# Attention with the keys on the partitions, transposed output, sums by additions and ones, a gate by tanh

## The chip, the cores and the metric

The kernel runs on one core of a Trainium2 chip. The time is the device time in microseconds (us) of that core; the median of several runs is quoted. Engine names in the profile: PE is TensorE's matmuls, PEld its weight loads, DVE is VectorE, ACT is ScalarE, POOL is GpSimd. "Cold" means that the profile shows TensorE's clock at half (0.50), "warm" at full (1.00). A "strip" is half of the rows or half of the columns of TensorE's array (64*128 or 128*64 in the profile, where the whole is 128*128). A "pass" is one streaming of 384 columns through the array, 0.16 us when warm (the p of the prediction): one for a bf16 matmul, four for an fp32 one, which runs as two parts of 0.32 us. Ratios of two kernels are the mean time of one kernel's fast runs over that of the other's fast runs of the same rounds, so they are not quite the ratio of the quoted medians.

## The reference

Two blocks in a row, all in fp32. Attention has 4 batches, 8 heads, 768 positions and 64 columns per head; a key counts for a query only if six sign bits of a projection agree:

```
q_bits = (einsum(q, proj) > 0);  k_bits = (einsum(k, proj) > 0)      # 6 bits each
mask   = bucket(q_bits) == bucket(k_bits)
scores = where(mask, q @ k.T / 8, -1e9)
attn   = exp(scores - max) / (sum + 1e-9)
x      = attn @ v                     # regrouped to 3072 tokens x 512
g = x @ w_gate;  val = x @ w_val      # 512 -> 1536
out = (g * sigmoid(g) * val) @ w_out  # 1536 -> 512
```

The three weights come as float64 and are rounded to fp32 on the chip ("narrowing": 36 pieces of 128 x 512, seven VectorE operations each).

## The kernel before

Heads are taken in pairs; a pair's q and k lie transposed with one head on partitions 0 to 63 and the other on 64 to 127. A unit of attention is 128 queries of one head, with the queries on the partitions. Its weights come out with queries on the partitions, so they must be turned (transposed) before they can be multiplied with the values, and the result must be turned again for the gated block. The mask is a matmul of the hash bits (bf16) added to the scores in PSUM.

```python
    def score(u):
        n, c, h = units[u]
        rows = slice(h * D, (h + 1) * D)
        ...
        for half in range(2):
            nc.tensor.matmul(sc[:, half, 0:HQ], bits["q", n][rows, qs], bits["k", n][rows, ks], start=True, stop=False)
            nc.tensor.matmul(sc[:, half, 0:HQ], T["q", n][rows, qs], T["k", n][rows, ks], start=False, stop=True)
        nc.vector.tensor_reduce(top, sc[:, :, 0:HQ], axis=AX.XY, op=ALU.max)
        ...  # scale and bias from top, two small operations
        nc.scalar.activation(A[u], sc[:, :, 0:HQ], AF.Exp, bias=bias, scale=scale, accum_out=sums[u])

    def turn(u):      # six transposes, copied out by VectorE and ScalarE
        ...
    def attend(u):    # six matmuls: turned weights stationary, 64 columns of values moving
        for i in range(NCH):
            nc.tensor.matmul(ps[:, 0:D], at[:, i, :], raws["v", n][:, h, i, :], start=i == 0, stop=i == NCH - 1)
        ...  # reciprocal of the sum, scaling
    def x_T(n, c):    # one transpose per two units, copied into xT
        ...
        # the gated block, per 128 of the 1536 columns
        def up(f):
            ...  # g and val: four fp32 matmuls of 384 columns each
            nc.scalar.copy(gs, g[:, 0:HQ])
            nc.scalar.activation(e, g[:, 0:HQ], AF.Exp, scale=-1.0)
            nc.vector.tensor_scalar(e, e, scalar1=1.0, scalar2=None, op0=ALU.add)
            nc.vector.reciprocal(e, e)
            nc.vector.tensor_tensor(gs, gs, e, op=ALU.mult)
            nc.vector.tensor_tensor(ht, gs, val[:, 0:HQ], op=ALU.mult)
```

Batch 0's attention runs while the weights are narrowed; the gated block of a batch runs in small pieces among the attention units of the next batch; the last batch's block stands alone at the end.

## Time and profile before

The median of before is 1792.73 us (1784.3 to 1793.24, three runs). I mark three stretches by the start of each batch's first g matmul:

| stretch of the profiled run | before, us |
|---|---|
| start to the first g (batch 0's attention, weights narrowed) | 385.5 |
| first g to the last batch's first g, per batch | 400.1 |
| last batch's first g to the end | 204.9 |

The sum 385.5 + 3 x 400.1 + 204.9 is the span of 1790.7. The last stretch still holds the end of attention in this kernel: a batch's block comes in two halves, and the second half of the last one starts at 1614.69. The prediction below shows the page's lines and reads them. The first stretch is cold nearly throughout, so a matmul removed there is worth about twice what it is worth later.

### The profile page before, as it was taken

What the parts mean: (1) busy time and instruction counts of PE and PEld (TensorE: products, weight loads), DVE (VectorE), ACT (ScalarE), POOL (GpSimd) and SP (SyncE); (2) the same over time, 40 slices, a digit from 0 to 9 for tenths busy, and PEclk for the clock granted to TensorE, in tenths of its full rate; (3) what the DMA queues carried; (4) which work ended last, traced back from release to release, by engine and by line L of the source; (5) the groups of instructions that cost most, each with busy time, mean ns of one, the idle gap of its engine ahead of it and who ended that gap; (6) DMA issues with size and microseconds to landing.
All of it is one profiled execution on the core that took longest, in us unless ns stands there. A gap on an engine that the chain in (4) does not pass through costs nothing.

```text
span 1790.7 us, 18403 instructions
## 1 busy us (share of the span) xinstructions
PE 1745.6 (97%) x7136; PEld 1111.1 (62%) x7136; DVE 1054.9 (59%) x2247; ACT 395.0 (22%) x793; POOL 19.8 (1%) x42
## 2 busy tenths in 40 slices
PE   6999999999999999999999999999999999999999
PEld 4677676766665666566665666566665666565454
DVE  6888887346652666346653666356653566256272
ACT  1111121112221222222221222122222222121010
POOL 0000000000000000000000000000000000000000
PEclk7555555569999999999999999999999899999999
DMA  5222221100001100020002000020001000000000
GB/s 143 84 80 77 80 77 36 27 1 10 1 1 47 25 1 1 12 51 10 0 1 62 10 1 1 12 51 10 1 6 39 1 1 0 12 7 0 18 1 18
DMA packets 63416, 45.23 MB, mean 25 GB/s; under 512 B 51552, under 2 KB 55648, under 8 KB 63328
## 3 DMA queue, kind: packets, MB, share of 16 engines
q1 hardware_dynamic: 58144, 25.18, 5.5%
q0 software_dynamic: 5184, 18.88, 3.6%
q8 instruction: 56, 0.92, 0.2%
q14 instruction: 32, 0.26, 0.1%
HBM read 37.75 MB, written 6.29 MB: 25 GB/s over the span
## 4 chain that ended last, share of the span: by engine, by line
PE 95%; DVE 2%; ACT 1%; issue 0%; DMA 0%; SPq 0%; ACTq 0%; DVEq 0%
PE av L241 17%; PE sc L206 16%; PE g L273 15%; PE po L289 14%; PE val L273 13%; PE aps L228 9%; PE sc L204 5%; PE hps L173 4%; PE tps L165 2%; PE xps L257 1%; ACT AT L234 1%; DVE e L280 1%; DMA kraw<-in_k_dram 0%; DVE ht L283 0%; DVE AT L232 0%
## 5 line engine op out<-in xcount | busy, mean ns | idle before, releaser
L241 PEld LDWEIGHTS av<-vraw,AT 128*128 128x128 f32 x2304 | 338.1, 224 | 70.9 <-issue 38.5
L206 PE MATMUL sc<-kT,qT 64*128 64x384 f32 x768 | 370.7, 569 | 0.0
L241 PE MATMUL av<-vraw,AT 128*128 128x64 f32 x2304 | 336.1, 305 | 2.6 <-DVE AT L232 2.6
L219 ACT ACTIVATE A<-sc,bias,scale 128x768 f32<-128x768 f32 x192 | 190.3, 991 | 618.4 <-DVE bias L215 528.0
L209 DVE TENSOR_REDUCE top<-sc 128x1 f32<-128x768 f32 x192 | 183.8, 958 | 192.6 <-PE sc L206 191.9
L273 PE MATMUL g<-xT,wg 128*128 128x384 f32 x768 | 272.6, 499 | 0.0
L273 PE MATMUL val<-xT,wv 128*128 128x384 f32 x768 | 263.4, 486 | 0.0
L289 PE MATMUL po<-wo,ht 128*128 128x512 f32 x576 | 250.8, 593 | 0.0
L280 DVE RECIPROCAL e<-e 128x384 f32<-128x384 f32 x96 | 245.1, 2553 | 3.3
L273 PEld LDWEIGHTS g<-xT,wg 128*128 128x128 f32 x768 | 144.2, 193 | 108.1 <-issue 23.3
L273 PEld LDWEIGHTS val<-xT,wv 128*128 128x128 f32 x768 | 146.1, 190 | 102.2 <-issue 0.9
L206 PEld LDWEIGHTS sc<-kT,qT 64*128 64x128 f32 x768 | 162.1, 222 | 56.3 <-issue 56.3
L228 PE MATMUL aps<-ident,A 128*128 128x128 f32 x1152 | 189.0, 309 | 3.1 <-ACT A L219 3.1
L289 PEld LDWEIGHTS po<-wo,ht 128*128 128x128 f32 x576 | 108.6, 190 | 132.5 <-issue 129.8
L248 DVE TENSOR_SCALAR xn<-av,r 128x64 f32<-128x64 f32 x192 | 54.5, 284 | 213.5 <-PE av L241 195.3
L234 ACT COPY AT<-aps 128x384 f32<-128x384 f32 x192 | 91.5, 477 | 402.0 <-PE aps L228 401.8
L279 DVE TENSOR_SCALAR e<-e 128x384 f32<-128x384 f32 x96 | 34.5, 360 | 231.3 <-ACT e L278 231.3
L228 PEld LDWEIGHTS aps<-ident,A 128*128 128x128 f32 x1152 | 161.2, 173 | 3.7 <-ACT A L219 3.7
L204 PE MATMUL sc<-kb,qb 64*128 64x384 bf16 x384 | 142.3, 371 | 0.2 <-DVE kb L178 0.2
L232 DVE COPY AT<-aps 128x384 f32<-128x384 f32 x192 | 105.8, 551 | 5.1 <-PE aps L228 3.9
L204 PEld LDWEIGHTS <-qb 64*128 64x128 bf16 x384 | 38.6, 100 | 72.1 <-issue 47.3
L276 ACT COPY gs<-g 128x384 f32<-128x384 f32 x96 | 45.9, 478 | 138.6 <-PE g L273 138.6
(59 smaller groups left out, 809.3 us busy)
## 6 DMA issues: line engine op xcount, KB each, us to landing
qraw<-in_q_dram SPq DMA_DIRECT2D x32, 192.0 KB, 3.5
words<-in_moe_w_gate_dram POOLq DMA_DIRECT2D x12, 512.0 KB, 3.8
kraw<-in_k_dram SPq DMA_DIRECT2D x32, 192.0 KB, 4.2
vraw<-in_v_dram SPq DMA_DIRECT2D x16, 384.0 KB, 4.0
words<-in_moe_w_val_dram POOLq DMA_DIRECT2D x12, 512.0 KB, 3.9
words<-in_moe_w_out_dram POOLq DMA_DIRECT2D x12, 512.0 KB, 3.8
out_dram<-o SPq DMA_DIRECT2D x24, 256.0 KB, 2.0
proj<-in_proj_dram SPq DMA_DIRECT2D x2, 1.5 KB, 3.4
```

Source lines behind the costliest of these rows:

```text
L173: nc.tensor.matmul(ps[:, 0:HQ], proj2, T[name, n][:, cols], start=True, stop=True)
L204: nc.tensor.matmul(sc[:, half, 0:HQ], bits["q", n][rows, qs], bits["k", n][rows, ks], start=True, stop=False)
L206: nc.tensor.matmul(sc[:, half, 0:HQ], T["q", n][rows, qs], T["k", n][rows, ks], start=False, stop=True)
L209: nc.vector.tensor_reduce(top, sc[:, :, 0:HQ], axis=AX.XY, op=ALU.max)
L219: nc.scalar.activation(A[u], sc[:, :, 0:HQ], AF.Exp, bias=bias, scale=scale, accum_out=sums[u])
L228: nc.tensor.transpose(ps[:, i * P : (i + 1) * P], a[:, half, i * P : (i + 1) * P], ident)
L232: nc.vector.tensor_copy(o, ps[:, 0:HQ])
L234: nc.scalar.copy(o, ps[:, 0:HQ])
L241: nc.tensor.matmul(ps[:, 0:D], at[:, i, :], raws["v", n][:, h, i, :], start=i == 0, stop=i == NCH - 1)
L273: nc.tensor.matmul(ps[:, 0:HQ], w[:, j, f * P : (f + 1) * P], x[:, j, :], start=j == 0, stop=j == NJ - 1)
L280: nc.vector.reciprocal(e, e)
L289: nc.tensor.matmul(ps[:, 0:DM], hs[f][:, i * P : (i + 1) * P], wo[:, f, :], start=f == 0, stop=f == NF - 1)
```

## The change

The keys go on the partitions. A unit is now 128 keys against 384 queries for both heads of a pair, so the weights come out as the values matmul needs them: no turning, and the output comes out transposed, as the gated block needs it. Sums of weights over the keys are additions on VectorE and one matmul with ones per head and half sequence. The row maximum is dropped. For queries that have no key in their bucket, two columns of ones stand beside the 384 columns of weights (hence 386 below): they give the plain sum of the values, which is added times a tiny constant and so decides the result only where all weights are zero. Finally the gate becomes 0.5 g (1 + tanh(g/2)). The two heads' matmuls now alternate between rows 0 to 63 and 64 to 127 (scores) and between output partitions 0 to 63 and 64 to 127 (values, sums).

```diff
 def score(u):
-    rows = slice(h * D, (h + 1) * D)
-    (queries stationary, keys moving, one head, two halves of the keys; row maximum; Exp with bias)
+    for x, start in ((bits, True), (T, False)):
+        for h in range(2):
+            rows = slice(h * D, (h + 1) * D)
+            nc.tensor.matmul(sc[:, h, 0:HQ], x["k", n][rows, ks], x["q", n][rows, qs],
+                             start=start, stop=not start)
+    nc.scalar.activation(ring[u % RING][:, :, 0:HQ], sc[:, :, 0:HQ], AF.Exp, scale=SCALE)
-def turn(u): ...        # gone
-def x_T(n, c): ...      # gone
 def attend(u):
+    for h in range(2):
+        nc.tensor.matmul(ps[h * D : (h + 1) * D, 0:AW], raws["v", n][:, h, c, :], a[:, h, :],
+                         start=c == 0, stop=c == NCH - 1)
+    (VectorE adds the weights of the six chunks of keys into acc)
+def norm(u):             # once per pair and half sequence
+    for h in range(2):
+        nc.tensor.matmul(ps[h * D : (h + 1) * D, 0:HQ], ones, t[:, h, :], start=True, stop=True)
+    (add, reciprocal, small constant, scale: four VectorE operations)
 up:
-    copy, Exp, add, reciprocal, two multiplications
+    nc.scalar.activation(t, ps[:, 0:HQ], AF.Tanh, scale=0.5)
+    nc.vector.scalar_tensor_tensor(out=t, in0=t, scalar=1.0, in1=ps[:, 0:HQ], op0=ALU.add, op1=ALU.mult)
+    nc.vector.scalar_tensor_tensor(out=ht, in0=now["t"], scalar=0.5, in1=ps[:, 0:HQ], op0=ALU.mult, op1=ALU.mult)
```

Cut: PSUM is shared out anew (two general banks instead of four, one for values, one for outputs), q and k copies move to ScalarE, output matmuls are queued in groups of three, and a batch's block is queued only when the whole batch is normalised.

More of the change, by code (lines that the diff above doesn't have):

```diff
@@ L49 @@
     OFF = 2.0**35
-    NONE = -(2.0**34)
     SCALE = 1.0 / D**0.5
+    EPS = 2.0**-100
     konst = ctx.enter_context(tc.tile_pool(name="konst", bufs=1))
@@ L55 @@
     opnd = ctx.enter_context(tc.tile_pool(name="opnd", bufs=2))
-    att = ctx.enter_context(tc.tile_pool(name="att", bufs=3))
-    small = ctx.enter_context(tc.tile_pool(name="small", bufs=4))
-    xp = ctx.enter_context(tc.tile_pool(name="xp", bufs=4))
+    att = ctx.enter_context(tc.tile_pool(name="att", bufs=2))
+    xp = ctx.enter_context(tc.tile_pool(name="xp", bufs=2))
     ffn = ctx.enter_context(tc.tile_pool(name="ffn", bufs=2))
@@ L62 @@
     sc_ps = ctx.enter_context(tc.tile_pool(name="sc_ps", bufs=2, space=PSUM))
-    mm_ps = ctx.enter_context(tc.tile_pool(name="mm_ps", bufs=4, space=PSUM))
+    av_ps = ctx.enter_context(tc.tile_pool(name="av_ps", bufs=1, space=PSUM))
+    po_ps = ctx.enter_context(tc.tile_pool(name="po_ps", bufs=1, space=PSUM))
+    mm_ps = ctx.enter_context(tc.tile_pool(name="mm_ps", bufs=2, space=PSUM))
     ctx.enter_context(tc.manual_schedule())
@@ L105 @@
     make_identity(nc, ident)
+    ones = konst.tile([P, D], FP32, tag="ones", name="ones")
+    nc.vector.memset(ones, 1.0)
+    RING = 4
+    AW = HQ + 2
+    ring = []
+    for i in range(RING):
+        t = konst.tile([P, 2, AW], FP32, tag=f"A{i}", name="A")
+        nc.gpsimd.memset(t[:, :, HQ:AW], 1.0)
+        ring.append(t)
     wg = konst.tile([P, NJ, DF], FP32, tag="wg", name="wg")
@@ L167, in transpose @@
                                     ident)
-            nc.vector.tensor_copy(T[name, n][:, half * HQ : (half + 1) * HQ], ps[:, 0:HQ])
+            nc.scalar.copy(T[name, n][:, half * HQ : (half + 1) * HQ], ps[:, 0:HQ])
         def hash_bits(name, half):
@@ L187, in front @@
         return steps
-    units = [(n, c, h) for n in range(len(pairs)) for c in range(NCH) for h in range(2)]
-    A = {}
-    sums = {}
-    AT = {}
-    xn = {}
+    units = [(n, half, c) for n in range(len(pairs)) for half in range(2) for c in range(NCH)]
+    acc = {}
+    av = {}
     xT = {}
     def score(u):
-        n, c, h = units[u]
-        rows = slice(h * D, (h + 1) * D)
-        qs = slice(c * P, (c + 1) * P)
+        n, half, c = units[u]
+        qs = slice(half * HQ, (half + 1) * HQ)
+        ks = slice(c * P, (c + 1) * P)
@@ L201, in score @@
         sc = sc_ps.tile([P, 2, 512], FP32, tag="sc", name="sc")
-        for half in range(2):
-            ks = slice(half * HQ, (half + 1) * HQ)
-            nc.tensor.matmul(sc[:, half, 0:HQ], bits["q", n][rows, qs], bits["k", n][rows, ks],
-                             start=True, stop=False)
-            nc.tensor.matmul(sc[:, half, 0:HQ], T["q", n][rows, qs], T["k", n][rows, ks],
-                             start=False, stop=True)
-        top = small.tile([P, 1], FP32, tag="top", name="top")
@@ L209, in score @@
-        nc.vector.tensor_reduce(top, sc[:, :, 0:HQ], axis=AX.XY, op=ALU.max)
-        scale = small.tile([P, 1], FP32, tag="scale", name="scale")
-        nc.vector.tensor_scalar(scale, top, scalar1=NONE, scalar2=SCALE,
-                                op0=ALU.is_gt, op1=ALU.mult)
-        bias = small.tile([P, 1], FP32, tag="bias", name="bias")
-        nc.vector.scalar_tensor_tensor(out=bias, in0=top, scalar=-1.0, in1=scale,
-                                       op0=ALU.mult, op1=ALU.mult)
@@ L217, in score @@
-        A[u] = att.tile([P, 2, HQ], FP32, tag="A", name="A")
-        sums[u] = small.tile([P, 1], FP32, tag="sum", name="sum")
-        nc.scalar.activation(A[u], sc[:, :, 0:HQ], AF.Exp, bias=bias, scale=scale,
-                             accum_out=sums[u])
-    def turn(u):
-        AT[u] = att.tile([P, NCH, P], FP32, tag="AT", name="AT")
-        a = A.pop(u)
-        for half in range(2):
-            ps = bank("aps")
-            for i in range(CH):
-                nc.tensor.transpose(ps[:, i * P : (i + 1) * P], a[:, half, i * P : (i + 1) * P],
-                                    ident)
-            o = AT[u][:, half * CH : (half + 1) * CH, :].rearrange("p c t -> p (c t)")
-            if half == 0:
-                nc.vector.tensor_copy(o, ps[:, 0:HQ])
-            else:
-                nc.scalar.copy(o, ps[:, 0:HQ])
@@ L236, in attend @@
-    def attend(u):
-        n, c, h = units[u]
-        at = AT.pop(u)
-        ps = bank("av")
-        for i in range(NCH):
-            nc.tensor.matmul(ps[:, 0:D], at[:, i, :], raws["v", n][:, h, i, :],
-                             start=i == 0, stop=i == NCH - 1)
-        r = small.tile([P, 1], FP32, tag="r", name="r")
-        nc.vector.tensor_scalar(r, sums.pop(u), scalar1=1e-9, scalar2=None, op0=ALU.add)
-        nc.vector.reciprocal(r, r)
-        if h == 0:
-            xn[n, c] = xp.tile([P, P], FP32, tag="xn", name="xn")
-        nc.vector.tensor_scalar(xn[n, c][:, h * D : (h + 1) * D], ps[:, 0:D], scalar1=r,
-                                scalar2=None, op0=ALU.mult)
@@ L251, in x_T @@
-    def x_T(n, c):
-        b, pr = pairs[n]
-        half, i = divmod(c, CH)
-        if (b, half) not in xT:
-            xT[b, half] = xp.tile([P, NJ, HQ], FP32, tag="xT", name="xT")
-        ps = bank("xps")
-        nc.tensor.transpose(ps[:, 0:P], xn.pop((n, c)), ident)
-        nc.vector.tensor_copy(xT[b, half][:, pr, i * P : (i + 1) * P], ps[:, 0:P])
-        if pr == NP - 1 and i == CH - 1:
-            push_ffn(b, half)
-    atoms = []
-    def push_ffn(b, half):
-        x = xT.pop((b, half))
-        hs = []
-        def up(f):
-            g, val = bank("g"), bank("val")
-            for w, ps in ((wg, g), (wv, val)):
-                for j in range(NJ):
-                    nc.tensor.matmul(ps[:, 0:HQ], w[:, j, f * P : (f + 1) * P], x[:, j, :],
-                                     start=j == 0, stop=j == NJ - 1)
-            gs = ffn.tile([P, HQ], FP32, tag="gs", name="gs")
-            nc.scalar.copy(gs, g[:, 0:HQ])
-            e = ffn.tile([P, HQ], FP32, tag="e", name="e")
-            nc.scalar.activation(e, g[:, 0:HQ], AF.Exp, scale=-1.0)
-            nc.vector.tensor_scalar(e, e, scalar1=1.0, scalar2=None, op0=ALU.add)
-            nc.vector.reciprocal(e, e)
-            nc.vector.tensor_tensor(gs, gs, e, op=ALU.mult)
-            ht = hp.tile([P, HQ], FP32, tag="ht", name="ht")
-            nc.vector.tensor_tensor(ht, gs, val[:, 0:HQ], op=ALU.mult)
-            hs.append(ht)
-        def down(i):
-            ps = bank("po")
-            for f in range(NF):
-                nc.tensor.matmul(ps[:, 0:DM], hs[f][:, i * P : (i + 1) * P], wo[:, f, :],
-                                 start=f == 0, stop=f == NF - 1)
-            o = ffn.tile([P, DM], FP32, tag="o", name="o")
-            nc.scalar.copy(o, ps[:, 0:DM])
-            rows = out[b * S : (b + 1) * S, :].rearrange("(p c) m -> p c m", c=NCH)
-            nc.sync.dma_start(rows[:, half * CH + i, :], o)
-        atoms.extend(lambda f=f: up(f) for f in range(NF))
-        atoms.extend(lambda i=i: down(i) for i in range(CH))
@@ new lines, in score, with attend @@
+        for x, start in ((bits, True), (T, False)):
[4 more added lines that the diff above has]
+        nc.scalar.activation(ring[u % RING][:, :, 0:HQ], sc[:, :, 0:HQ], AF.Exp, scale=SCALE)
+    def attend(u):
+        n, half, c = units[u]
+        a = ring[u % RING]
+        if c == 0:
+            av[n, half] = av_ps.tile([P, 512], FP32, tag="av", name="av")
+        ps = av[n, half]
+        for h in range(2):
+            nc.tensor.matmul(ps[h * D : (h + 1) * D, 0:AW], raws["v", n][:, h, c, :], a[:, h, :],
+                             start=c == 0, stop=c == NCH - 1)
+        if c == 1:
+            acc[n, half] = att.tile([P, 2, HQ], FP32, tag="acc", name="acc")
+            nc.vector.tensor_tensor(acc[n, half], ring[(u - 1) % RING][:, :, 0:HQ],
+                                    a[:, :, 0:HQ], op=ALU.add)
+        elif c > 1:
+            nc.vector.tensor_tensor(acc[n, half], acc[n, half], a[:, :, 0:HQ], op=ALU.add)
+        if c == NCH - 1:
+            av[n, half] = att.tile([P, AW], FP32, tag="avs", name="avs")
+            nc.scalar.copy(av[n, half], ps[:, 0:AW])
@@ new lines, in norm @@
+    def norm(u):
+        n, half, _ = units[u]
+        b, pr = pairs[n]
+        if pr == 0 and half == 0:
+            xT[b] = xp.tile([P, NP, S], FP32, tag="xT", name="xT")
+        ps = bank("sum")
+        t = acc.pop((n, half))
+        for h in range(2):
+            nc.tensor.matmul(ps[h * D : (h + 1) * D, 0:HQ], ones, t[:, h, :], start=True, stop=True)
+        a = av.pop((n, half))
+        r = att.tile([P, HQ], FP32, tag="r", name="r")
+        nc.vector.tensor_scalar(r, ps[:, 0:HQ], scalar1=S * EPS, scalar2=None, op0=ALU.add)
+        nc.vector.reciprocal(r, r)
+        e = att.tile([P, 1], FP32, tag="e", name="e")
+        nc.vector.tensor_scalar(e, a[:, HQ : HQ + 1], scalar1=EPS, scalar2=None, op0=ALU.mult)
+        nc.vector.scalar_tensor_tensor(out=xT[b][:, pr, half * HQ : (half + 1) * HQ],
+                                       in0=a[:, 0:HQ], scalar=e, in1=r,
+                                       op0=ALU.add, op1=ALU.mult)
+        if pr == NP - 1 and half == 1:
+            push_ffn(b)
@@ new lines, with push_ffn, up, down @@
+    atoms = []
+    def push_ffn(b):
+        x = xT.pop(b)
+        for half in range(2):
+            cols = slice(half * HQ, (half + 1) * HQ)
+            hs = []
+            now = {}
+            def up(f, w, name, x=x, cols=cols, now=now, hs=hs):
+                ps = bank(name)
+                for j in range(NJ):
+                    nc.tensor.matmul(ps[:, 0:HQ], w[:, j, f * P : (f + 1) * P], x[:, j, cols],
+                                     start=j == 0, stop=j == NJ - 1)
+                if name == "g":
+                    t = ffn.tile([P, HQ], FP32, tag="t", name="t")
+                    nc.scalar.activation(t, ps[:, 0:HQ], AF.Tanh, scale=0.5)
+                    nc.vector.scalar_tensor_tensor(out=t, in0=t, scalar=1.0, in1=ps[:, 0:HQ],
+                                                   op0=ALU.add, op1=ALU.mult)
+                    now["t"] = t
+                else:
+                    ht = hp.tile([P, HQ], FP32, tag="ht", name="ht")
+                    nc.vector.scalar_tensor_tensor(out=ht, in0=now["t"], scalar=0.5,
+                                                   in1=ps[:, 0:HQ], op0=ALU.mult, op1=ALU.mult)
+                    hs.append(ht)
+            def down(i, fs, now=now, hs=hs, half=half):
+                if fs[0] == 0:
+                    now["o"] = po_ps.tile([P, DM], FP32, tag="po", name="po")
+                ps = now["o"]
+                for f in fs:
+                    nc.tensor.matmul(ps, hs[f][:, i * P : (i + 1) * P], wo[:, f, :],
+                                     start=f == 0, stop=f == NF - 1)
+                if fs[-1] == NF - 1:
+                    o = ffn.tile([P, DM], FP32, tag="o", name="o")
+                    nc.scalar.copy(o, ps)
+                    rows = out[b * S : (b + 1) * S, :].rearrange("(p c) m -> p c m", c=NCH)
+                    nc.sync.dma_start(rows[:, half * CH + i, :], o)
+            for f in range(NF):
+                atoms.append(lambda f=f, up=up: up(f, wg, "g"))
+                atoms.append(lambda f=f, up=up: up(f, wv, "val"))
+            for i in range(CH):
+                for f in range(0, NF, 3):
+                    atoms.append(lambda i=i, f=f, down=down: down(i, range(f, f + 3)))
@@ L303 @@
     per = 2 * NCH
-    rate = 2 * (NF + CH) / (NP * per - 2)
+    rate = 2 * (2 * NF + CH * NF // 3) / (NP * per - 4)
     credit = 0.0
@@ L316 @@
                 narrow(u)
-            if at == 10 and n + 2 < len(pairs):
+            if at == per - 1 and n + 2 < len(pairs):
                 load(n + 2)
@@ L322 @@
             atoms.pop(0)()
-        if 2 <= u < N + 2:
-            attend(u - 2)
         if 1 <= u < N + 1:
-            turn(u - 1)
-        if u >= 3 and units[u - 3][2] == 1:
-            x_T(*units[u - 3][:2])
+            attend(u - 1)
+        if u >= 3 and units[u - 3][2] == NCH - 1:
+            norm(u - 3)
     for atom in atoms:
```

## The prediction

> **What bounds the kernel now.** I read the page first (busy shares, clock row, chain of waits), then the stretches of time, then the timeline of TensorE in one warm and one cold spot, then the groups by line.
>
> ```profile
> span 1790.7 us, 18403 instructions
> ...
> PE 1745.6 (97%) x7136; PEld 1111.1 (62%) x7136; DVE 1054.9 (59%) x2247; ACT 395.0 (22%) x793; POOL 19.8 (1%) x42
> ...
> PEclk7555555569999999999999999999999899999999
> ...
> PE 95%; DVE 2%; ACT 1%; issue 0%; DMA 0%; SPq 0%; ACTq 0%; DVEq 0%
> PE av L241 17%; PE sc L206 16%; PE g L273 15%; PE po L289 14%; PE val L273 13%; PE aps L228 9%; PE sc L204 5%; PE hps L173 4%; PE tps L165 2%; PE xps L257 1%; ACT AT L234 1%; DVE e L280 1%; DMA kraw<-in_k_dram 0%; DVE ht L283 0%; DVE AT L232 0%
> ```
>
> TensorE is busy 97% and holds 95% of the chain that ended last. So only TensorE work, or TensorE's clock, is worth time. 57% of the chain is attention and its preparation, 42% the gated block. The clock row shows two stages:
>
> ```profile
> 200.00:300.00 100.00, 100.00 (x331) 71.09 (x332) 82.68 (x191) 19.80 (x38) 5.82 (x11) 0.50 0.25 71
> ...
> 500.00:900.00 400.00, 392.20 (x1789) 248.22 (x1788) 228.38 (x497) 99.04 (x200) 0.00 (x0) 1.00 0.07 16
> ```
>
> (Columns: stretch, its length, busy us of TensorE, its weight loads, VectorE, ScalarE, GpSimd, then clock, DMA share, GB/s.) Up to about 388 us, batch 0, attention runs alone at half clock, with VectorE at 83% because it also narrows the weights. After that the gated block is mixed in, the clock is full and VectorE idles at 57%. One warm unit (128 queries of one head) without a piece of the block:
>
> ```profile
> 542.32 0.33 PE L204 MATMUL sc<-kb,qb 64*128 64x384 bf16 x1
> 542.50 0.81 PE L206 MATMUL sc<-kT,qT 64*128 64x384 f32 x2
> 543.14 0.32 PE L204 MATMUL sc<-kb,qb 64*128 64x384 bf16 x1
> 543.30 0.80 PE L206 MATMUL sc<-kT,qT 64*128 64x384 f32 x2
> 544.04 0.55 PE L165 MATMUL tps<-ident,kraw 128*128 128x128 f32 x3
> 544.42 1.45 PE L241 MATMUL av<-vraw,AT 128*128 128x64 f32 x12
> 545.71 0.83 PE L228 MATMUL aps<-ident,A 128*128 128x128 f32 x6
> 546.47 0.33 PE L204 MATMUL sc<-kb,qb 64*128 64x384 bf16 x1
> ```
>
> Differences of starts (durations overlap, so they don't add): scores 1.72 us, three transposes of k 0.38, weights times values 1.29, turning of weights 0.76. A bf16 pass of 384 columns is 0.16-0.18; an fp32 one is two matmuls of 0.32, so 0.64. And the cold end of batch 0:
>
> ```profile
> 382.16 0.50 PE L204 MATMUL sc<-kb,qb 64*128 64x384 bf16 x1
> 382.45 1.48 PE L206 MATMUL sc<-kT,qT 64*128 64x384 f32 x2
> 383.73 0.52 PE L204 MATMUL sc<-kb,qb 64*128 64x384 bf16 x1
> 384.05 1.48 PE L206 MATMUL sc<-kT,qT 64*128 64x384 f32 x2
> 385.47 5.14 PE L273 MATMUL g<-xT,wg 128*128 128x384 f32 x8
> 390.44 2.74 PE L273 MATMUL val<-xT,wv 128*128 128x384 f32 x8
> 393.02 1.45 PE L241 MATMUL av<-vraw,AT 128*128 128x64 f32 x12
> ```
>
> The same scores take 3.31 us. The first eight dense matmuls still run cold (4.97), the next eight warm (2.58): density, not busy time, raised the clock.
>
> **What the Trainium skill says.** (1) "TensorE: Matmul & The Clock Gate", Part 3, The mechanism: matmuls in different row or column strips of the array overlap, and a weight load overlaps a running matmul only if its row group differs; matmuls still start in order. It measures 3.07x for four row tiles and 2.38x for three column tiles. Before puts both score halves in one head's rows, so its trace cannot show this. (2) "TensorEngine Tiling (Array Packing)", Key Properties: changing the tiling mode drains the engine. The trace fits: the four score matmuls should stream 1.60 us and cost 1.72 up to the next kind. (3) The clock-gate page, Part 1, says about 3.4 us of sustained work gives the full clock. The trace differs: TensorE is 100% busy at 0.50 for over 300 us, so busy time alone is not what counts. (4) "ScalarE: Activation LUTs", Table sets: exp and tanh share a set, so tanh should not bring table loads. Before has one load (1.28 us), only exp and copies; nothing in it tests tanh.
>
> **The change, part by part.** There are 192 units before and after. A new unit is 128 keys of both heads against 384 queries.
>
> *TensorE removed:* six turnings per unit, 192 x 0.76 = 146 us at full clock; the transposes of x, 96 x about 0.2 = 19; the wait of 0.62 in front of most of these (ScalarE's copy), some 15 per batch. Weights times values goes from 12 short matmuls (64 columns each, paced by loads) to four of 386 columns: 4 x 0.32 = 1.29, the same if they run one after the other.
>
> *TensorE added:* ones times sums, two fp32 passes per half pair: 8 x 1.29 = 10 us a batch.
>
> *Overlap, the open term:* scores now go head 0, head 1 in rows 0-63 and 64-127, different banks. In units of p = 0.16 us: bits 0 and 1 together 1p; head 0 first part 2p; its second part beside head 1's first 2p; head 1's second 2p: 7p = 1.12 instead of 10p = 1.60. Weights times values in two column halves: 6p instead of 8p, 0.97 instead of 1.29. An fp32 matmul's two parts use the same strip, hence not a full halving.
>
> *A later batch:* the block is 24 x 2 x 2.58 = 124 plus six outputs x 10.30 (24 matmuls in the chain) = 62, together 186, unchanged. Fronts 16 x 0.38 + 16 x 0.75 = 18. Check on before: 48 x 3.77 + 18 + 5 + 15 + 186 = 405, and it measures (1612 - 388) / 3 = 408. After, with 0.1 us per score and 0.05 per attend for drains: with overlap 48 x (1.22 + 1.02) + 8 + 18 + 186 = 320; without, 48 x (1.71 + 1.34) + 10 + 18 + 186 = 360. Waits on top: the single output bank makes the next output wait for its 0.585 us copy, 6 x about 0.8 = 5, and about 5 that I can't place: 330 or 370.
>
> *VectorE:* gone are the row maximum (192 x 958 ns = 184 us), four tiny operations per unit (120), the copies of turned weights (106), xn and xT (82), q and k copies (35, to ScalarE), and the gate's chain (34 + 245 + 54 of its four operations):
>
> ```profile
> L209 DVE TENSOR_REDUCE top<-sc 128x1 f32<-128x768 f32 x192 | 183.8, 958 | 192.6 <-PE sc L206 191.9
> ...
> L280 DVE RECIPROCAL e<-e 128x384 f32<-128x384 f32 x96 | 245.1, 2553 | 3.3
> ```
>
> New: 160 additions of 768 columns at about 0.96 (384 take 0.558; 400 ns more at the same rate) = 153; 32 normalisations of 0.55 + 2.55 + 0.16 + 0.56 = 3.82 = 122; 96 extra first gate steps, 53. From 1055 to about 575. None of it was on the path in later batches, so it pays only in batch 0.
>
> *Batch 0:* narrowing is 4.1 us per unit for 36 units (timeline, 201.16 to 205.28). VectorE per unit: 4.1 + 0.8 + 0.65 + 0.25 (hash bits) = 5.8. TensorE cold: 2.4 + 2.0 + 0.75 + 0.33 = 5.5 with overlap, 3.3 + 2.6 + 0.75 + 0.44 = 7.1 without. So 22 (first loads) + 36 x 5.9 + 12 x 5.5 = 300 with overlap; 22 + 48 x 7.1 = 363 without. If the clock comes up: 268 or 277, VectorE bound for 36 units either way.
>
> *Tail:* the last batch's block can start only when both halves are normalised, so all 186 lie behind attention (before: 1614.7 to the end, 176). Ahead of it lies a bare chain: addition 0.96, ones 1.3, normalisation 3.8, hand-overs: 7; then a first cold group, 2 (before: 4.44 instead of 2.74), and the last copy and store, 4. About 199.
>
> *Sum:* with overlap 300 + 3 x 330 + 199 = 1489; without, 363 + 3 x 370 + 199 = 1672.
>
> **Rivals.** (a) No overlap: 1672, 7% faster. For it: fp32 in two parts with its own loads, and nothing in the trace proves overlap. I give it 30%; partial overlap (scores only, about 1590) 20%. (b) VectorE becomes the bound: true for 36 units of batch 0, already counted; later it needs about 2.3 us per unit of 6.9, so no. (c) The clock: batch 0's array is fuller now, so it may warm, which takes 30 to 85 us off; but it may be cold for the four units between two batches' blocks where no block work is queued (72 pieces over 44 of 48 units), at most 10 us each, 30. (d) Two shared banks instead of four stall the gate: g's bank needs tanh 0.5 and one VectorE step 0.55, and val's 2.58 us cover it. Against this speaks only a normalisation (3.8 us) in VectorE's queue, 8 per batch: up to 8 x 2 x 3 = 48 in all. (e) tanh forces table loads: up to 96 x 2 x 1.28 = 246 us on ScalarE, which is 22% busy, so mostly hidden; 30 us at worst.
>
> **Range and chances.** Weighting 1489 (50%), 1590 (20%), 1672 (30%) gives 1564; a clock that may come up in batch 0 (about even, -50) pulls to about 1535, and I say 1530. The range 1430 to 1660 spans overlap with a warm batch 0 (1457, less some waits that I may have overstated) to no overlap cold, nearly. Even (a) with 50 us of extra stalls is 4% faster, so faster is 0.97.
>
> **What would show it.** Overlap: starts of a warm unit's scores spread over 1.12-1.22 us instead of 1.6-1.7, attend's over about 1.0. Batch 0: VectorE above 90% until about 235 us, the first g at 270-300 (360 if no overlap), clock row 0.5 or not there. Later batches 330 us apart; VectorE near 35% in them. One table load. The tail: first g to the end about 190, with a TensorE gap of about 7 us ahead. It is wrong if later batches stay near 400 us, if TensorE waits more than 3% in them for the two shared banks, or if drains between three tiling modes eat the saved turnings.

## The result, and the profile after

The changed kernel takes 1332.53 us (1332.16 to 1333.82, four runs); the ratio to before is 0.7446, 95% interval 0.7427 to 0.7465. The direction was right, but 1332 lies 98 us below the range of 1430 to 1660: the prediction was wrong, by being too cautious.

The page of the changed kernel: span, busy shares, the busy tenths and clock in 40 slices, and the chain that ended last.

```profile
span 1331.9 us, 10961 instructions
...
PE 1224.7 (92%) x4480; PEld 557.7 (42%) x4480; DVE 551.4 (41%) x840; ACT 257.0 (19%) x409; POOL 20.0 (2%) x46
...
PE   5645556999999999999999999999999999999998
...
DVE  5999997543224433343224433333224432320110
...
PEclk9875767999999999999999999999999999999999
...
PE 81%; DVE 15%; issue 2%; DMA 1%; ACT 1%; POOL 0%; ACTq 0%; POOLq 0%; DVEq 0%
PE po L294 19%; PE g L274 19%; PE val L274 18%; PE sc L217 10%; PE av L228 9%; PE hps L187 3%; PE tps L179 2%; DVE acc L235 2%; DVE r L252 2%; PE sum L248 1%; DVE x L158 1%; DVE x L155 1%; DMA words<-in_moe_w_gate_dram 1%; DVE wo L157 1%; DVE wv L157 1%
```

TensorE is about half idle in the first seven slices, in most of which VectorE is full, and at 90% or more after that up to the last. VectorE now holds 15% of the chain (before: 2%), nearly all of it in batch 0. The chain's share of scores and values fell from 38% (17 + 16 + 5) of 1791 us to 19% of 1332, about 680 to 250 us. The stretches of the changed kernel, with the columns that the prediction explains:

```profile
22.00:228.00 206.00, 121.47 (x489) 39.84 (x487) 195.21 (x321) 39.25 (x60) 17.54 (x34) 0.72 0.35 106
228.00:249.00 21.00, 21.00 (x113) 7.43 (x112) 14.06 (x19) 8.76 (x13) 0.00 (x0) 1.00 0.15 38
...
545.00:840.00 295.00, 293.14 (x1098) 135.07 (x1094) 101.57 (x143) 61.37 (x99) 0.00 (x0) 1.00 0.07 19
...
1138.00:1332.00 194.00, 187.07 (x530) 99.91 (x528) 30.27 (x52) 15.30 (x30) 0.00 (x0) 1.00 0.02 8
```

Up to 228 us VectorE is 95% busy and TensorE 59%; TensorE's clock averages 0.72 because it goes up and down. From 228 us TensorE is always busy, at full clock. In a later batch VectorE stands at 34% (101.57 of 295), as predicted. Warm units without a piece of the block, in TensorE's timeline (start, length, what):

```profile
241.57 0.34 PE L217 MATMUL sc<-qb,kb 64*128 64x384 bf16 x2
241.75 0.81 PE L217 MATMUL sc<-qT,kT 64*128 64x384 f32 x4
242.48 0.87 PE L228 MATMUL av<-A,vraw 128*64 128x386 f32 x4
243.29 0.34 PE L217 MATMUL sc<-qb,kb 64*128 64x384 bf16 x2
```

Read from start to start: scores 242.48 - 241.57 = 0.91 us (predicted 1.22 with overlap, 1.71 without), values 243.29 - 242.48 = 0.81 (predicted 1.02 or 1.34). Four fp32 parts of 0.32 each fit into 0.73, and the two bf16 matmuls into 0.18. That is a full halving, not the partial one I had allowed. The end of narrowing on VectorE, and the seam to the last batch's block on TensorE:

```profile
17.84 0.42 DVE L149 TENSOR_SCALAR wg<-words 128x512 int32<-128x512 int32 x1
```

```profile
214.53 0.69 DVE L159 SCALAR_TENSOR_TENSOR wo<-x,wo 128x512 f32<-128x512 int32 x1
215.13 2.01 DVE L235 TENSOR_TENSOR acc<-acc,A 128x768 f32<-128x768 f32 x2
```

```profile
1134.35 0.34 PE L217 MATMUL sc<-qb,kb 64*128 64x384 bf16 x2
1134.53 0.81 PE L217 MATMUL sc<-qT,kT 64*128 64x384 f32 x4
1135.26 0.87 PE L228 MATMUL av<-A,vraw 128*64 128x386 f32 x4
1136.31 0.87 PE L228 MATMUL av<-A,vraw 128*64 128x386 f32 x4 [0.17 <-ACT A L219]
1137.30 0.87 PE L248 MATMUL sum<-acc,ones 128*64 128x384 f32 x4
1138.10 2.85 PE L274 MATMUL g<-xT,wg 128*128 128x384 f32 x8
```

Narrowing runs from 17.84 to 215.13: 36 units of 5.48 us. At the end there is no gap of 7 us before the last block: the g matmuls start right after the ones matmul, long before the last normalisation is done. The block's first half reads only queries of the first half, which were normalised six units earlier.

The other waits that the prediction feared, from the groups of the changed kernel (busy and mean ns, then idle before and its releaser):

```profile
L294 PE MATMUL po<-wo,ht 128*128 128x512 f32 x576 | 258.9, 597 | 6.9 <-ACT o L298 6.9
...
L182 ACT ACT_TABLE_LOAD x1 | 1.3, 1283 | 0.7 <-PEq L354 0.7
```

All outputs together waited 6.9 us for their single bank, and there is one table load although Exp and Tanh alternate. The stretches side by side (the three later batches are 299.4, 299.4 and 290.2 after, the last without a next batch to prepare; 401.2, 399.0 and 400.2 before):

| stretch | before | after | predicted, with overlap and cold |
|---|---|---|---|
| to the first g | 385.5 | 249.1 | 300 |
| per later batch | 400.1 | 296.3 | 330 |
| last first g to the end | 204.9 | 193.8 | 199 |

### The profile page after: what moved, and what is told of

Read it like the earlier page. It is cut to its first block, busy times and chain, and to the rows that moved or that the text cites. A ratio compares the mean times of both kernels' runs of the same rounds, so it can differ in the third digit from the quotient of the medians.

```text
span 1331.9 us, 10961 instructions
## 1 busy us (share of the span) xinstructions
PE 1224.7 (92%) x4480; PEld 557.7 (42%) x4480; DVE 551.4 (41%) x840; ACT 257.0 (19%) x409; POOL 20.0 (2%) x46
## 4 chain that ended last, share of the span: by engine, by line
PE 81%; DVE 15%; issue 2%; DMA 1%; ACT 1%; POOL 0%; ACTq 0%; POOLq 0%; DVEq 0%
PE po L294 19%; PE g L274 19%; PE val L274 18%; PE sc L217 10%; PE av L228 9%; PE hps L187 3%; PE tps L179 2%; DVE acc L235 2%; DVE r L252 2%; PE sum L248 1%; DVE x L158 1%; DVE x L155 1%; DMA words<-in_moe_w_gate_dram 1%; DVE wo L157 1%; DVE wv L157 1%
## 5 line engine op out<-in xcount | busy, mean ns | idle before, releaser
L219 ACT ACTIVATE A<-sc 128x768 f32<-128x768 f32 x192 | 155.9, 812 | 567.3 <-PE sc L217 406.9
L228 PE MATMUL av<-A,vraw 128*64 128x386 f32 x768 | 176.6, 540 | 32.5 <-ACT avs L238 25.2
L280 DVE SCALAR_TENSOR_TENSOR t<-t,g 128x384 f32<-128x384 f32 x96 | 53.2, 555 | 332.5 <-ACT t L279 332.5
L217 PE MATMUL sc<-qT,kT 64*128 64x384 f32 x768 | 164.3, 508 | 0.0
L235 DVE TENSOR_TENSOR acc<-acc,A 128x768 f32<-128x768 f32 x128 | 122.0, 953 | 55.0 <-ACT A L219 53.8
L285 DVE SCALAR_TENSOR_TENSOR ht<-t,val 128x384 f32<-128x384 f32 x96 | 53.1, 554 | 161.8 <-PE val L274 161.8
L279 ACT ACTIVATE t<-g 128x384 f32<-128x384 f32 x96 | 47.2, 491 | 320.7 <-PE g L274 320.7
L252 DVE RECIPROCAL r<-r 128x384 f32<-128x384 f32 x32 | 81.7, 2553 | 1.1
L217 PEld LDWEIGHTS sc<-qT,kT 64*128 64x128 f32 x768 | 73.5, 201 | 0.2 <-issue 0.2
L217 PE MATMUL sc<-qb,kb 64*128 64x384 bf16 x384 | 67.0, 346 | 0.0
```

Of the source, the lines that this page charges most:

```text
L217: nc.tensor.matmul(sc[:, h, 0:HQ], x["k", n][rows, ks], x["q", n][rows, qs], start=start, stop=not start)
L219: nc.scalar.activation(ring[u % RING][:, :, 0:HQ], sc[:, :, 0:HQ], AF.Exp, scale=SCALE)
L228: nc.tensor.matmul(ps[h * D : (h + 1) * D, 0:AW], raws["v", n][:, h, c, :], a[:, h, :], start=c == 0, stop=c == NCH - 1)
L235: nc.vector.tensor_tensor(acc[n, half], acc[n, half], a[:, :, 0:HQ], op=ALU.add)
L252: nc.vector.reciprocal(r, r)
L279: nc.scalar.activation(t, ps[:, 0:HQ], AF.Tanh, scale=0.5)
```

## The experiments

Theory A: the two heads run fully side by side in their strips of the array; the turning is gone at its full price; VectorE's narrowing bounds batch 0. The rivals were P (the prediction's half overlap, from strict program order), R (strips don't matter, the gain is the turning, the clock or VectorE's relief) and others stated at each run. All experiments were timed in four runs each. Those that give a wrong result do the same amount of work as the kernel they are taken from, except where work is taken away or its form is changed.

### 1. Scores of both heads in one row strip (wrong result)

```diff
-                rows = slice(h * D, (h + 1) * D)
+                rows = slice(0, D)
```

> The changed kernel with both heads' score matmuls on rows 0 to 63 (wrong result on purpose, same work). Theory A, the two heads' scores run fully side by side in the two row strips: a unit's scores go from 0.91 us back to ten passes, about 1.71, so 144 x 0.80 = 115 us in the later batches plus about 10 at the end of batch 0: 1455 us (1435 to 1475). Theory P, the half overlap of the prediction (7 passes): 144 x 0.48 = 69 plus 6: 1407. Rival R, the gain is the turning and the clock, strips don't matter: within 1% of 1332.

Measured: 1455.42 us, on theory A's number. A warm unit in TensorE's timeline:

```profile
249.68 0.49 PE L217 MATMUL sc<-qb,kb 64*128 64x384 bf16 x2
250.02 1.45 PE L217 MATMUL sc<-qT,kT 64*128 64x384 f32 x4
251.40 0.87 PE L228 MATMUL av<-A,vraw 128*64 128x386 f32 x4
```

The same six matmuls now take 251.40 - 249.68 = 1.72 us, as the ten passes of a unit did before the change (542.32 to 544.04 in the prediction's lines). A later batch is 333.1 us instead of 296.3: +36.8 for 48 units.

### 2. Values of both heads in one column strip (wrong result)

```diff
         for h in range(2):
-            nc.tensor.matmul(ps[h * D : (h + 1) * D, 0:AW], ...
-                             start=c == 0, stop=c == NCH - 1)
+            o = h * D if c == 0 else 0
+            nc.tensor.matmul(ps[o : o + D, 0:AW], ...
+                             start=c == 0, stop=(c == NCH - 1 and h == 1) or (c == 0 and h == 1))
```

The first of the six chunks of keys (c == 0) keeps its two strips, so five of six units are serial. A larger constant is added to the sums so that the wrong numbers stay finite.

> The changed kernel with both heads' weights-times-values in columns 0 to 63 for five of six chunks (wrong result on purpose). Theory A: attend of such a unit from 0.80 to 1.44 us, 120 x 0.64 = 77 plus about 7 in batch 0: 1416 us (1400 to 1430). Theory P (6 passes instead of 8): 120 x 0.32 plus 4: 1374. Rival R: within 1% of 1332.

Measured: 1412.73 us, again A. A serial unit's values and the next scores in TensorE's timeline:

```profile
246.25 1.51 PE L229 MATMUL av<-A,vraw 128*64 128x386 f32 x4
247.69 0.34 PE L217 MATMUL sc<-qb,kb 64*128 64x384 bf16 x2
```

The values take 247.69 - 246.25 = 1.44 us, and a later batch is 321.2 us, +24.9.

### 3. Both in one strip (wrong result)

> Both undone together: the changed kernel without any strip overlap except in the sums. Theory A with a clock that still comes up in batch 0: 1332 + 125 + 84 = 1541. Theory A with batch 0 cold throughout (TensorE then needs about 7.1 us a unit there and is the bound again): up to 1640. The later batches alone should be (115 + 77) / 3 = 64 us longer than 296 each. Rival R: 1332 to 1350.

Measured: 1536.7 us. A later batch is 358.4, +62.1, the sum of the two (61.7). Batch 0 grew only to 265.7: the clock came up there too (0.86, the third number from the end), so the cold branch did not come about.

```profile
22.00:228.00 206.00, 165.46 (x482) 65.15 (x481) 195.09 (x322) 40.10 (x60) 17.54 (x34) 0.86 0.35 104
```

The overlap taken away here is worth 1536.7 - 1332.5 = 204 us; the overlap in the sums and in one values chunk of six is still there.

### 4. Head by head

Only the program order of a unit's score matmuls changes; the result is right.

```diff
-        for x, start in ((bits, True), (T, False)):
-            for h in range(2):
+        for h in range(2):
+            for x, start in ((bits, True), (T, False)):
```

> Only the program order of the four score matmuls of a unit changed: all of head 0, then all of head 1 (right result). If matmuls start strictly in program order, overlap is only at the seam: 8 passes, 1.38 instead of 0.91 us, 144 x 0.47 = 68 plus 6: 1406 us. If the two strips run through their matmuls without regard to the order between them: 1332, within 1%.

Measured: 1333.23 us, no change. The built program has this order on TensorE (a listing without times, weight loads left out):

```
Matmult sc<-qb,kb    head 0, bf16
Matmult sc<-qT,kT    head 0, fp32 (two parts)
Matmult sc<-qb,kb    head 1, bf16
Matmult sc<-qT,kT    head 1, fp32 (two parts)
```

The weight loads of a unit start in that order too (in the changed kernel both bf16 loads come first, then the four fp32 ones):

```profile
241.36 0.09 PEld L217 LDWEIGHTS <-kb 64*128 64x128 bf16 x1 [0.60 <-issue]
241.37 0.20 PEld L217 LDWEIGHTS sc<-qT,kT 64*128 64x128 f32 x1
241.37 0.09 PEld L217 LDWEIGHTS <-kb 64*128 64x128 bf16 x1
241.38 0.36 PEld L217 LDWEIGHTS sc<-qT,kT 64*128 64x128 f32 x3
```

The matmuls themselves run like this:

```profile
241.36 0.34 PE L217 MATMUL sc<-qb,kb 64*128 64x384 bf16 x2
241.54 0.82 PE L217 MATMUL sc<-qT,kT 64*128 64x384 f32 x4
242.28 0.87 PE L228 MATMUL av<-A,vraw 128*64 128x386 f32 x4
```

Both bf16 matmuls, 0.333 us each, lie within 0.34 us: head 1's starts beside head 0's, ahead of head 0's fp32 matmul, which stands before it in the program. So within a unit's scores each row strip works through its own matmuls, and the order between the strips does not hold one back for the other. This is the point on which the prediction's seven and six passes rested; the same exchange of order was not run for the values, where the trace shows only that they take four passes.

### 5. Narrowing by one operation of seven (wrong weights)

> The changed kernel with one of the seven narrowing operations kept (weights wrong on purpose). Theory A: VectorE's narrowing bounds batch 0 (36 units of 5.48 us), the rest of the kernel is untouched. Then VectorE needs about 0.45 + 1.5 us a unit and batch 0 falls to TensorE: 48 units of about 2.2 us at full clock, first g at 17 + 106 = 125 to 150 instead of 249, 1215 to 1235 in all; if the clock is at half all through batch 0, 4.3 us a unit, first g near 225, 1308. Rival: batch 0 is bound by loads or by TensorE: 1332 within 1%.

Measured: 1238.8 us, 94 less; the first g comes at 155.8 instead of 249.1 and everything after it is as it was (3 x 296.3 and 193.8). So VectorE's narrowing was the bound of batch 0. The time is 4 us over my range, and the page's chain shows why:

```profile
PE 87%; DMA 6%; issue 3%; DVE 3%; ACT 1%; POOL 0%; POOLq 0%; ACTq 0%; DVEq 0%
PE po L284 20%; PE g L264 20%; PE val L264 20%; PE sc L207 11%; PE av L218 10%; PE hps L177 3%; DMA words<-in_moe_w_val_dram 2%; DMA words<-in_moe_w_out_dram 2%; PE tps L169 2%; DMA words<-in_moe_w_gate_dram 2%; PE sum L238 1%; DVE r L242 1%; ACT o L288 1%; DVE acc L225 0%; DVE acc L222 0%
```

With VectorE out of the way the loading of the weights (6% of the chain, as "words") takes its place for part of batch 0.

### 6. Before without the turning (wrong result)

In before, the weights go into the values matmul unturned: six transposes and two copies per unit are gone, everything else stays.

```diff
-        at = AT.pop(u)
+        at = A.pop(u).rearrange("p h (c t) -> p (h c) t", t=P)
...
-        if 1 <= u < N + 1:
-            turn(u - 1)
```

> The kernel before without the turning of weights: the weights go into the values matmul as they are (wrong result on purpose, same shapes), so the six transposes and the two copies are gone, all else stays. Theory A: worth 0.76 us a unit at full clock, 144 x 0.76 = 109, and 1.42 at half clock, 48 x 1.42 = 68, plus waits for ScalarE's copy of up to 15 a batch: 1792 - 177 - 0..45 = 1570 to 1615. If the turning kept batch 0 cold, its clock comes up too and batch 0 is shorter by up to another 100. Rival (the turning hides beside weight loads): above 1700.

Measured: 1595.59 us, in the range. Batch 0 fell by 60 us to 325.7, a later batch by 43.9 to 356.2. The guess that the turning kept batch 0 cold is wrong: its clock stays at 0.50 from 21.9 us on for 307 us.

### 7. Before with a light VectorE

In before, the gate by tanh, and no row maximum.

```diff
-        nc.vector.tensor_reduce(top, ...)      # and the two small operations after it
-        nc.scalar.activation(A[u], ..., AF.Exp, bias=bias, scale=scale, accum_out=sums[u])
+        nc.scalar.activation(A[u], ..., AF.Exp, scale=SCALE, accum_out=sums[u])
...        # up: Tanh and two scalar_tensor_tensor, as in the change
```

> The kernel before with the gate by tanh and without the row maximum and its three small followers (a few queries without a key come out wrong): VectorE is relieved of about 184 + 120 + 280 us, TensorE's work is as before. Theory A: VectorE wasn't on the path, so 1775 to 1792, at most 1% faster. Rival (VectorE's load is where the gain comes from): 1600 or less. One table load if exp and tanh share a set.

(The expectation counts three followers of the maximum; the edit removes two.) Measured: 1746.91 us, ratio 0.976 (0.9728 to 0.9793). This missed my range of 1775 to 1792: the relief was worth 2.4%. It didn't come from batch 0 (first g at 381.0 instead of 385.5) but from the later batches, 387.9 instead of 400.1. TensorE's waits in before begin

```profile
PE xps L257 <- ACT AT L234: 23.7, 38, 0.6
PE tps L165 <- DMA qraw<-in_q_dram: 9.1, 1, 9.1
PE aps L228 <- ACT A L219: 3.1, 1, 3.1
PE av L241 <- DVE AT L232: 2.6, 7, 1.7
```

and in this kernel

```profile
PE tps L165 <- DMA qraw<-in_q_dram: 9.1, 1, 9.1
PE av L232 <- DVE AT L223: 3.5, 1, 3.5
PE xps L248 <- DVE xn L239: 0.4, 1, 0.4
```

The 23.7 us in front of x's transposes are gone. They are put down to ScalarE's copy of turned weights, which this kernel still has; but the edit relieves both engines, VectorE from 1055 to 552 us and, by the gate's copy, ScalarE from 395 to 328, so which of the two reliefs ended the waits isn't shown. Experiment 6, which takes that copy away, has none of these waits either. Before also has two dips to half clock in its later part (10.2 and 3.4 us long, so about 7 us lost); this kernel has none. That names 31 of the 45 us; the rest I can't place. The one table load came true. In before, then, the relief is worth a tenth of the gain of 460; in the changed kernel, where TensorE has less to do, it may be worth more, and no run tests that.

### 8. Seventeen narrowings later

```diff
-            if u < len(pieces):
-                narrow(u)
+            late = 17
+            early = len(pieces) - late
+            if u < 48 and u * early // 48 != (u - 1) * early // 48:
+                narrow(u * early // 48)
+            elif 48 <= u < 48 + late:
+                narrow(early + u - 48)
```

> The changed kernel with 17 of the 36 narrowings moved from batch 0 into the first 17 units of batch 1, where VectorE is about a third busy (right result). Theory A: batch 0 is bound by VectorE, so it is 17 x 4.05 = 69 us shorter less what then shows of TensorE, batch 1 grows by at most 20: 1265 to 1300. Rival (batch 0 bound by something else, or batch 1 takes it all back): 1320 or more.

Measured: 1272.51 us, ratio to before 0.7108, with a right result: 60 us (4.5%) faster than the change, and the fastest right kernel. The first two stretches:

```profile
22.00:177.00 155.00, 123.08 (x599) 42.22 (x595) 149.15 (x233) 49.08 (x74) 10.60 (x20) 0.91 0.36 99
177.00:487.00 310.00, 300.79 (x1121) 137.47 (x1122) 161.57 (x252) 63.82 (x102) 6.89 (x13) 0.99 0.15 43
```

The first g comes at 177.4, 72 us earlier. Batch 1 takes 309.5 instead of 299.4 us: it absorbs 17 narrowings (VectorE goes from 34% to 52%) and gives back 10.

### 9. Short values matmuls again (wrong result)

This and the next ask why batch 0 stayed at half clock before and not after. Values go back to twelve short parts, weights stationary and 64 columns moving (cut: the copy of the values and the constant added to the sums are fitted to the new form):

```diff
-            nc.tensor.matmul(ps[h * D : (h + 1) * D, 0:AW], raws["v", n][:, h, c, :], a[:, h, :], ...)
+            for i in range(CH):
+                o = (h * CH + i) * D
+                nc.tensor.matmul(ps[:, o : o + D], a[:, h, i * P : (i + 1) * P],
+                                 raws["v", n][:, h, c, :], start=True, stop=True)
```

> What brought the clock up in batch 0: the changed kernel with weights times values again as six short matmuls a unit (weights of 128 queries as the stationary operand, 64 columns of values moving, twelve parts), wrong result on purpose; scores, sums and narrowing as in the changed kernel. Theory H1: short matmuls paced by their weight loads don't count as enough activity, and that kept the kernel before cold. Then batch 0 stays at 0.50 from about 25 us until the first g, TensorE takes about 1.8 + 2.6 + 0.75 + 0.33 = 5.5 us a unit there, first g at 280 to 300; later batches 48 x (1.29 - 0.80) = 24 us longer: 1332 + 40 + 72 = 1430 to 1460. Theory H2: the form of the values matmul doesn't matter for the clock: it alternates as in the changed kernel (mean about 0.7 in batch 0), first g at 255 to 265, 1410 to 1420.

Measured: 1411.28 us, first g at 252.8, the clock alternates with a mean of 0.65 between 22 and 228 us. H1 falls: short values matmuls alone don't keep it at half to the first g.

### 10. Short values and one strip (wrong result)

The edits of 1 and 9 together.

> Both earlier edits together: six short values matmuls a unit and both heads' scores in one strip, so TensorE's stream in batch 0 is that of the kernel before without its turning (wrong result on purpose). Theory H3: the clock follows how much of the array streams, and only the two together leave too little. Then batch 0 stays at 0.50 to the first g, TensorE needs 3.3 + 2.6 + 0.75 + 0.33 = 7.0 us a unit, first g at 340 to 355, later batches 296 + 28 + 37 = 361, in all 1620 to 1640. Rival H4 (what TensorE streams doesn't decide it; that VectorE makes TensorE pause does): the clock comes up at times, first g at 265 to 285, 1540 to 1565.

Measured: 1614.86 us, first g at 346.3; the first g is in H3's range, the whole 5 us below it. The clock row of this kernel,

```profile
PEclk9555555569999999999999999999999999999999
```

and that of experiment 3, where the same scores in one strip go with long values matmuls:

```profile
PEclk9988889999999999999999999999999999999999
```

Here the clock fell at 47 us and stayed at 0.50 for 304 us, although TensorE was always busy:

```profile
200.00:300.00 100.00, 100.00 (x294) 65.64 (x293) 46.09 (x72) 15.12 (x22) 2.47 (x8) 0.50 0.12 33
```

So how busy TensorE is doesn't decide it: in the changed kernel the stretch from 228 to 249 us is also 100% busy and runs at full clock. What it streams matters: in all four kernels that stayed cold (before, experiments 6, 7 and 10) the cold spell ends 3.4 to 4.7 us after the first g matmul starts, with no pause of TensorE in between. Which quantity is measured stays open. Common to the four are scores in one strip together with short values matmuls; either one alone (experiments 1 and 3; 9) let the clock come up. That this means "too little of the array streams at a time" (H3) is not shown, and one pair of runs speaks against its simplest form: experiment 3, which also puts the values in one strip, was warmer between 22 and 228 us (0.86) than experiment 1 (0.67).

## Why the prediction was wrong, point by point

**Right in mechanism.** TensorE was the bound, and its work was what the change was worth; the turning, the overlap of heads, VectorE as the bound of 36 units of batch 0, one table load, an unchanged block at the end. In a later batch the parts add up: 400.1 less the turning (43.9, experiment 6) and less the strips (61.7, experiments 1 and 2) is 294.5, and the changed kernel has 296.3. That it closes so well is partly luck, for five terms of 3 to 7 us are left out and nearly cancel: values take 1.44 us in one strip where before they took 1.29 (48 x 0.15 = +7); the ones matmuls come (8 x 0.75 = +6); the transposes of x go (24 x 0.2 = -5); the relief of VectorE and ScalarE counts as far as experiment 6 did not bring it too (12 less 7.5 of waits and 2 of clock dips, -3); and experiment 2 left the overlap of one unit in six (8 x 0.63 = -5).

**The step that failed: "An fp32 matmul's two parts use the same strip, hence not a full halving".** From starts in program order I worked out 7 passes for the scores and 6 for the values. They take 5 and 4: 0.91 and 0.81 us with the hand-over, not 1.22 and 1.02. Experiment 4 shows the reason, for the scores: the order between strips does not bind. Per later batch this is 48 x (0.31 + 0.21) = 25 us, and 2 more in the sums. The other 7 of the 34 us are mostly waits: I had put 10 on each batch, and few came (TensorE idles 1.9 of the 299.4 us of a batch, the outputs' wait for their bank being 1.4 of it).

**The chances: 30% for no overlap and 20% for part of it.** They moved my figure from 1489 (overlap) towards 1672 and, less what I allowed for a warm batch 0, to 1530: 41 us of the miss of 198. The other 157 is 51 in batch 0, 3 x 34 in the later batches and 5 at the end. Rival (a) is refuted by experiments 1 to 3. With nearly all overlap undone (experiment 3) the change still takes 1537, not 1672: mostly because rival (a) also assumed a cold batch 0 (363 against 265.7), the rest because its later batches are shorter too (358 against 370).

**Batch 0: "22 + 36 x 5.9 + 12 x 5.5 = 300".** The first part was right in kind and slightly too long: narrowing began at 17.8 and ran 5.48 us a unit, ending at 215 instead of 234. The second part was wrong: the rest took 34 us instead of 66, because the clock was up by then (1.00 from 223 us) and the overlap was complete. The prediction had the warm clock as a branch (268), about even; for this part it was the one that came, while the VectorE-bound part averaged 0.72. Even that branch was 19 us too long.

**The end: "All 186 lie behind attention ... a bare chain".** The block is queued late, but its first half needs nothing of the last normalisation. The gap of 7 us and the cold first group did not come; small waits of the outputs for their bank (2.9 us here) took part of that back, 193.8 against 199.

**Rivals (c), (d), (e).** The cold stretch between two batches' blocks didn't come (the clock is 1.00 from 223 us to the end). The two shared banks don't stall TensorE visibly in the later batches, where it is 99% busy. Tanh brought no table load.

**Readings and sums that don't hold, though the range doesn't rest on them.** The check "(1612 - 388) / 3 = 408" runs from a first half's block to a second half's; from first g to first g a batch is 400.1. The wait in front of x's transposes is not "some 15 per batch" but 7.5 (22.4 us in 36 waits over the three batches); with that the check's own sum is 397.5. VectorE's sum doesn't close: 1055 less the 860 listed plus the 328 new is 523, not 575; measured 551. And the 57% at which VectorE "idles" is its busy share.

**Where the gain of 460 us is.** 136 in batch 0, 311 in the three later batches, 11 at the end. The 11 at the end are no faster block: before's 204.9 hold 29 us of attention (up to 1614.69), the changed kernel's 193.8 none. Batch 0's 136 is the largest single stretch. There a cold TensorE was the bound; now VectorE is, and experiments 5 and 8 show that the next 60 to 94 us lie there.

## What to carry to other kernels

When a contraction or an output is only half the array wide, put two independent matmuls next to each other in different strips: here two heads took about the time of one, in fp32 too (scores 0.91 us instead of 1.72, values 0.81 instead of 1.44), and the scores did so in either program order. Before trusting a busy share of 97% as a floor, ask whether the work could share the array and at which clock it ran. And when TensorE's work shrinks, look at once at what else runs in that stretch: here a one-time preparation on VectorE became the bound and could be moved to where VectorE had slack.

## What the Trainium skill lacked or had wrong

- "TensorE: Matmul & The Clock Gate", Part 3, The mechanism, says that matmuls start and end strictly in program order. Starts did not, across two row strips: with the program order head 0 bf16, head 0 fp32, head 1 bf16, both bf16 matmuls (0.333 us each) fit into 0.34 us ahead of the fp32 ones, and the kernel took 1333 us where in-order starts would by my estimate have made it 1406. The order of ends was not tested.
- The same part has no figure for two strips with fp32 operands in two parts: ten passes took the time of five (1.72 to 0.91 us with the hand-over) in row strips, eight that of four (1.44 to 0.81) in column strips.
- The same page, Part 1, ties the clock to how busy TensorE is. Busy time, as this profile shows it, doesn't decide it: before was 100% busy at 0.50 for most of a 369 us spell at half clock, experiment 10 likewise in one of 304 us, while experiment 3, 80% busy (165.46 of 206 us), averaged 0.86.
- "TensorEngine Tiling (Array Packing)", Key Properties, says that a change of tiling mode drains the engine, without a figure. Here a unit's scores took 0.11 us and its values 0.16 us more than their streams (0.91 against 5 x 0.16, 0.80 to 0.81 against 4 x 0.16); how much of that is the drain wasn't measured apart.
